# A new order of the same instructions in the five queues of a linear-attention and gMLP block

## The chip, the cores and the metric

The kernel runs on one core of one Trainium2 chip. The metric is the device time of one execution in microseconds (us), the median over runs. All times below are in us unless ns is written. The engines are PE (TensorE, matrix products), DVE (VectorE), ACT (ScalarE), POOL (GpSimd) and SP (SyncE, which here only issues DMAs).

## The reference

A residual block of linear attention is followed by a residual block of a spatial gMLP, in bf16. The sequence has 2048 rows of 512; 32 heads of 16; the gMLP is 1792 wide, in two halves of 896.

```
phi(t) = where(t > 0, t + 1, exp(t)) + 1e-6
q, k, v = heads(LN(x) @ wqkv);  pq, pk = phi(q), phi(k)
kv  = einsum('bhsd,bhse->bhde', pk, v);  z = sum over s of pk
o   = einsum('bhqd,bhde->bhqe', pq, kv) / (einsum('bhqd,bhd->bhq', pq, z) + 1e-6)
h   = x + o @ wo
u   = gelu(LN(h) @ w_in);  z1, z2 = u[:, :896], LN(u[:, 896:])
g   = w_sp @ z2 + b_sp            # 2048 x 2048 over the sequence
out = h + (z1 * g) @ w_out
```

## The kernel before, in words

**Program and order.** The kernel is written as a list of 1143 steps. A step is one instruction of DVE, ACT or POOL, one DMA issue, or a group of matmuls on PE. The helpers `matmuls`, `act`, `dve`, `pool`, `dma` and `dma_t` (a DMA that transposes) append steps; for each step the tiles that it reads and writes give the steps that must come before it. The order in which each engine runs its steps is not the order in which the code appends them. It stands in the constant `ORDER` (L16), a packed list of the 1143 step numbers written by an offline search. `schedule()` unpacks it and splits it by engine into five queues; each engine runs its queue strictly in order. `emit()` goes through the queues and writes, ahead of each step, the semaphore waits that its dependencies need and that no earlier step of the same engine has covered. So a step that waits holds up all that stand behind it on its engine. Because a helper records many steps, many rows of the profile have the helper's line: L413 is any group of matmuls, L432 any ACT instruction, L443 and L446 any load and any DMA transpose, L849 any sum of blocks (`comb`), L852 any `add_on`.

**SP's queue.** Of the 122 entries of SP's queue most are transposes (tiles of the normalized x into `xt6` to `xt15`, of the normalized h into `ht0` to `ht15`, of the spatial weights into `wt0` to `wt15` in two halves each, of the gated products into `zg0` to `zg15`). The others are loads (half of x, the wq, wv, wo, win2, win1 and wout weights), spreads of the reciprocals (`r`, in pieces) and stores (`o`). One `dma_t` occupies SP for some 1.2 to 1.3 us.

**Stages.** Times are those of the profiled execution.

- 0 to 8: loads of x, warm-up of PE.
- 8 to 50: attention. `k_unit` takes two tiles of 128 rows: statistics on DVE (`stats`), reciprocal root on POOL (`rstd`), `norm` on DVE or ACT (L566), transposes (on PE for tiles 0 to 5, on SP's queue for 6 to 15), the K projection and `phi` (an exp on ACT, then min and add, then max on DVE), and the accumulation of pk with xn (L670). `q_unit` does the same for 512 columns of Q (L413, then `phi`). Each of the two keeps its projections in pairs of PSUM banks.
- 43 to 61: the accumulated state `ct`, its product with wv (PE L753), the mask `kvm` (DVE L757) and the product with wo (`m`, L764). The denominators go through zc on PE, Ln and Exp on ACT, the spreads r on SP and the multiplication of pqT on DVE (L803). Four groups of 512 rows, tg = 0 to 3, follow each other.
- 57 to 72: h = x + pqT·m (DVE L815), squares on ACT, moments of a pair of tiles on POOL (`moments_pair`: L553 to L557), norm on DVE (L566), transposes ht on SP.
- 67 to 109: the first layer of the gMLP. `cell3` multiplies 2 x 2 blocks with seven products instead of eight: sums of weight blocks (`w_sums`: four for win2, four for win1), sums of blocks of hn (`hn_sums`), adds in PSUM by `add_on` (DVE L852) and gelu on ACT. z2 is normalized (moments on POOL at L545 to L548, the power at L561 or `rstd` at L529, norm at L566); `t1_sums` and `t_sums` make zt of it. `z1_tile` and `cell2` do the other half.
- 106 to 215: `mix`, eight times, is the spatial product with wt, again by seven products, with sums sa and wt (DVE L849), gate products (L984, L992) and the zg transposes. `cell2` lies between the first of them and `mo_pair`, the output product with wout (adds into h at DVE L1077), beside the later ones.
- 215 to 228.4: the last `mo_pair` and the stores.

Of the kernel before, what the change touches and what calls it, by code (L numbers as in the profile page):

```python
# [11 lines left out]
P = 128  # L12
GRAN = 16
EARLY = 0
SEM_NS = 45.0
ORDER = "c-jrpg8~@j0tV0z|7_c~ZQHhOw_44tc{SU%QA5qPS6j`h*4DPRd!ON)Scr|d0EqaAgXBmFBOQbkNRNObNQH<fh6pH%49JKyh=<}xi!4Zh)F^?HNQkT`g-j@ovdE0=sD*5(gSIG#D9C}j$c5UdhcZZnoG6d>$c+j}jQYrf{K$)TsE7{eh<s>(0;q&eXox~+jDo0)LFkM|Xo4h&jsX~mu4sxc&<s`41<g?fg)ta4&>ht<8A(wcU!ogoVj_B=1-`=9n1YsQg`PNqNf?4;n2KJQhC^71p@@nZ=#4)327NIdtuYL3FdWOV0wb^rt1%uwV<x`GNQ}Z^tid>}#X9uEFBpwkn1KG6gQNHX8!;Q3@GaJ31Lop5V&FT>!znDrd_=+`9K#qa!C0KYX)Hx#Y{nLx#2;9Ot$2uC*oNKMjy+g_g?NPhIDozQ5&Q5H&f*{*;|$JW2X^8-uHXVL;|4C`Dz4!YZXzb0;1;gqC7$9}+{P>1!9CnXWd4R|c!3RkjVSyR&#;DT`5YVh7veA~|3ggP$KQy{7<_<__y_A4oxdX<qwx(s{lCIHB;>zH%C~qAGZEu6Hk0u)K0u7c<Rk-=Fe0-v2MaI)3o-#CF(=EgBy%wp6SELgGdEK(9m}#5YcM5ivnJCs16MH(OS2A}GcEJ5F!M4qi?AH?u_(*46}xdIv#=O5F(d0TKP#{WTeBj2vO6oW7AvzQi?bf<vjlsv7ppNFzhoO`WdnZAZ}<;;^Dz5xJcsftwq;*7WOdGBI}YJ@Y|kp3z;F2@8?ghAa4vslKlbNrPUIX`<s>#`N6zCg4(BiYiEnv_T{xe&c#OAsh)3Cs$9b2(@*PKT0T=QFf8#+8;39TqW8ULQuIFOj=L25gQ@-a#PG%>b;w3)gM^53t9LdXU!p(fn!}`F^yuxI9LFfx!r9>syRQ|_N%%>z8%+VZ6>oX%LseWgEjbTbH;W$RrKt@tf3Kh^a{=rW?%~YDsmpsGNimX@~#2=VOv2~W26-C#$l-F5Ag%n3|^^gTsN`;k0Gx&;GHIvy?LQ%Dx#S~4=R8p_mTm#ia15{M;lwIf8RHap1W%WJNY8h9srM57>a;S_Rv4zU%F%zhjHnF^JFr5bJD^*u|B~%9GR0XwGbPds9-DDeeRz+=P4Sk_5%BAznsG9ndnY4|S^cUwVx4P<UeW_aNrbK$e;rd3qG*p#UTMM*P!!%cUG)i@}TYs~PMrwriXr9_CvEFdB_9}*AYC9LHyT)je7HS9Esje0)ua;<^R&%V{>zXEOsn)22Zm5T@>!zw|ijHWR#%ZeRsi$tKmu~Bw)@q&ZXuNi^nwIOJrs)^$VsG8mdfn3mb<}k2=C}G)^|e7W^qc<G3T@PPy01-Ypq2VwKj?S;p?|bloitNhG*Mf%hY$5YhxAx|v`UZkvsUYg`s$cY>ZqQopJu6{-U{BPy?m~He5MonsL$H27dox|Jgzf(ua}yw*E+xtqW7zjPN|6h(*>3AC!Ll2N`I=cF6x}@+Aiuj+M(dTRmcbQM*UUH#U06)bx9HYmm)isuPBCNI<^b@N1azmM|C{Maa>1n8ULjCPT)k2=!8z}22SGAj^?DU<4#WI<WA{wPT`uqs#N~P^<Bzoo!YgW#$|oPbsgR5T-hC*-WgrR8C>2KoXORk#T9+WSzXVKebAYm&4--bRbAaV+|ZqU!uNd49evVAeabm~#;4uLz1+mdoy&LK&0XBohyAm2`>b2JtGoN0&%1`d@d)?yNMG^=S8^Wbbu(XaK40`@_i<~t^)-L*fBe=xeAPpI)4%$<o4cJyxwqRmzkl<65A`iS@Ie3Juie7K{m66N*T4IrAA7X>`H7!-ko)_oUwD`c_y^DSbHDOS|LcN&=W%}R_a5vIUgy8v(qsIm2lz|3_eB5YkN#wY|NPkuF~e9-_ZObz%?=@Ah#daU6=r$7qlCC2LWmt^c&_7xSRqn~9-@T_jvqF8o)d?J;kIWwPFU{*AyG&YrZ{<+?1i4{ubeSt4oSl_rwrfvjW;-1ND~%0bx09Xg{)zXvxRgaeaIBPbIGvQ*+Y(yGc5KpZ*-Qh)wx5ikSEOd4lj59P%z{TMMB}Q(yN>=6bOaFHm`8;P&zDesj%G(yxLn_CKL;0L%Fcm4MX{`&pTZqR1OtGrBEdt@P6-djIi5P!wnY=)x%Qnam~;;Gz!(ikFF7#gxcXJ*9mn))KDv=4JAU;&@9vs^+JQtJoF4LLd(!Pv<iJfo6sw?4ShrV&@prgokP3OA!G=hLjTY`bPK)1fG{xh3tdBx@IT`6A!q"  # L16


class _Op:
# [13 lines left out]
class _Prog:  # L33
# [110 lines left out]
    def schedule(self):  # L144

        ids = np.frombuffer(zlib.decompress(base64.b85decode(ORDER)), np.uint16).tolist()
        assert len(ids) == len(self.ops)
# [981 lines left out]
```

## Time and profile before

| what | value |
|---|---|
| median of three runs | 230.19 us (229.83, 230.19, 230.55) |
| profiled execution | 230.16 us |
| its span in the trace | 228.4 us |
| outside the span | 1.76 us |
| granted PE clock | 1.00 throughout |
| transposes xnT<-xn, hnT<-hn, from issue to landing | 2.5 us, both (median) |
| load of win, 896 KB | 8.8 us (median of two) |
| spreads r<-rcp | 2.7 us |

The span is the time between the first and the last instruction of the program in the trace. A row of the timeline has the start in us, the length in us, the engine, the line, the operation, then the tile written and the tiles read with their sizes and, in brackets, how long the engine stood idle before it and what released it. The chain of waits is read back from the last instruction: at each step, what released it, or the instruction ahead of it on its engine. PE's idle time in it counts; that of an engine off the chain does not.

### The profile page before, as it was taken

The numbers are of one execution on the slowest core, as the hardware profiler recorded it, in microseconds if no ns is written. First come the engines' busy times: TensorE is split into PE (matmuls) and PEld (weight loads), VectorE is DVE, ScalarE is ACT, GpSimd is POOL, SyncE is SP. The second block draws the span as 40 slices with busy tenths as digits, with TensorE's granted clock in tenths as the row PEclk, the third lists the DMA queues.
The fourth block names the chain that finished last, engine by engine and source line by source line (L and its number), as shares of the span: only waits on it lengthen the run. The fifth ranks groups of instructions, "written<-read, shape, count | busy, mean of one in ns | idle before, by whom it ended". The sixth has DMA issues, their size and how long they took to land.

```text
span 228.4 us, 3524 instructions
## 1 busy us (share of the span) xinstructions
PE 221.4 (97%) x1253; PEld 115.3 (50%) x1253; DVE 177.8 (78%) x397; ACT 123.3 (54%) x232; POOL 49.7 (22%) x134
## 2 busy tenths in 40 slices
PE   7999999999999998999999999999999999999995
PEld 7444444453344443544545455555655556655553
DVE  3999656689999998999999955638877677553973
ACT  5794663489999998998654234425202213222111
POOL 2533600000567735595800000000000000000000
DMA  7725439957463337799980291249893150170664
GB/s 216 244 49 138 71 72 324 257 112 181 100 134 68 69 72 93 147 184 198 228 121 0 40 109 20 42 81 148 188 193 64 43 108 19 28 78 0 149 160 153
DMA packets 73905, 26.85 MB, mean 118 GB/s; under 512 B 63648, under 2 KB 73888, under 8 KB 73888
## 3 DMA queue, kind: packets, MB, share of 16 engines
q1 hardware_dynamic: 73184, 26.03, 56.0%
q10 hardware_dynamic: 704, 0.59, 0.8%
q8 instruction: 10, 0.16, 0.4%
q14 instruction: 7, 0.06, 0.1%
HBM read 6.95 MB, written 2.10 MB: 40 GB/s over the span
## 4 chain that ended last, share of the span: by engine, by line
PE 63%; DVE 12%; DMA 7%; ACT 7%; SPq 6%; POOL 3%; issue 2%; DVEq 0%
PE psum L413 57%; SPq L446 6%; PE psum L670 4%; DMA hnT<-hn 2%; DMA wt<-in_B_w_sp_dram 2%; DMA xnT<-xn 2%; ACT z L432 1%; DMA x<-in_A_x_dram 1%; DVE st L929 1%; DVE h L1077 1%; DVE pqT L803 1%; DVE h L815 1%; ACT xn L432 1%; ACT sq L432 1%; DVE psum L852 1%
## 5 line engine op out<-in xcount | busy, mean ns | idle before, releaser
L432 ACT ACTIVATE psum<-psum 128x448 f32<-128x448 f32 (+1 forms) x49 | 22.1, 464 | 57.7 <-PE psum L413 35.7
L413 PE MATMUL psum<-z,wt 128*128 128x448 bf16 x256 | 53.0, 353 | 0.0
L413 PEld LDWEIGHTS psum<-z,wt 128*128 128x128 bf16 x256 | 24.8, 98 | 22.1 <-DVE wt L849 0.6
L413 PE MATMUL psum<-win,hnT 128*128 128x448 bf16 x112 | 26.0, 352 | 1.0 <-DMA hnT<-hn 1.0
L413 PE MATMUL psum<-zt,sa 128*128 128x448 bf16 x128 | 26.7, 352 | 0.0
L432 ACT ACTIVATE z1t<-psum 128x448 bf16<-128x448 f32 (+1 forms) x24 | 16.1, 676 | 17.9 <-PE psum L413 17.2
L432 ACT ACTIVATE e<-psum 128x1024 bf16<-128x1024 f32 (+1 forms) x18 | 16.7, 927 | 13.1 <-PE psum L413 12.4
L852 DVE TENSOR_TENSOR psum<-psum,p5z 128x448 f32<-128x448 f32 x24 | 14.9, 624 | 5.8 <-ACT z1t L432 5.1
L413 PE MATMUL psum<-ws,hs 128*128 128x448 bf16 x72 | 18.9, 353 | 0.0
L413 PEld LDWEIGHTS psum<-zt,sa 128*128 128x128 bf16 x128 | 12.4, 98 | 11.0 <-DVE zt L849 0.4
L413 PEld LDWEIGHTS psum<-win,hnT 128*128 128x128 bf16 x112 | 10.8, 98 | 11.6 <-ACT z1t L432 1.7
L413 PE MATMUL psum<-wout,zgT 128*128 128x256 bf16 (+1 forms) x77 | 15.1, 302 | 0.8 <-DVE h L1077 0.7
L413 PE MATMUL psum<-xnT,wqkv 128*128 128x512 bf16 x64 | 15.5, 379 | 0.0
L984 DVE SCALAR_TENSOR_TENSOR z1t<-psum,b,z1t 128x448 bf16<-128x448 f32 x16 | 10.8, 682 | 5.8 <-PE psum L413 5.8
L413 PE MATMUL psum<-wqkv,xnT 128*128 128x512 bf16 x64 | 15.0, 379 | 0.2 <-DMA xnT<-xn 0.2
L432 ACT ACTIVATE z<-psum 128x896 bf16<-128x896 f32 x16 | 14.8, 944 | 0.6 <-PE psum L413 0.6
L670 PE MATMUL psum<-pk,xn 128*128 128x512 bf16 x64 | 15.1, 379 | 0.0
L413 PE MATMUL psum<-m,pqT 128*128 128x512 bf16 x64 | 14.6, 380 | 0.2 <-DVE h L815 0.2
L992 DVE TENSOR_TENSOR u<-psum,p 128x448 bf16<-128x448 f32 x16 | 9.9, 623 | 5.2 <-PE psum L413 5.1
L545 POOL TENSOR_SCALAR st<-st 128x1 f32<-128x1 f32 x10 | 4.2, 419 | 44.5 <-ACT sh L432 35.2
L592 DVE TENSOR_SCALAR e<-e 128x1024 bf16<-128x1024 bf16 (+1 forms) x18 | 7.2, 400 | 8.3 <-ACT e L432 8.1
L413 PE MATMUL psum<-zt,wt 128*128 128x448 bf16 x64 | 13.4, 352 | 0.0
(124 smaller groups left out, 384.4 us busy)
## 6 DMA issues: line engine op xcount, KB each, us to landing
r<-rcp SPq DMA_DIRECT2D x16, 128.0 KB, 2.7
out_dram<-h SPq DMA_DIRECT2D x15, 128.0 KB, 2.0
win<-in_B_w_in_dram SPq DMA_DIRECT2D x2, 896.0 KB, 8.8
x<-in_A_x_dram SPq DMA_DIRECT2D x6, 256.0 KB, 3.6
wqkv<-in_A_wqkv_dram SPq DMA_DIRECT2D x2, 512.0 KB, 4.4
wout<-in_B_w_out_dram SPq DMA_DIRECT2D x1, 896.0 KB, 6.5
wo<-in_A_wo_dram SPq DMA_DIRECT2D x1, 512.0 KB, 5.4
wt<-in_B_w_sp_dram SPq DMA_TRANSPOSE x32, 4.2
```

The lines of the kernel that those rows point to most:

```text
L413: inst = pe.matmul(out_ap, lhsT=a, rhs=b, start=start and i == 0, stop=stop and i == len(pairs) - 1, **kw)
L432: return g.add("ACT", lambda ac: ac.activation(out_ap, in_ap, func, **kw), [in_ap, *extra], [out_ap] + ([accum] if accum is not None else []),
L446: return g.add("SP", lambda q: q.dma_start_transpose(out_ap, in_ap), [in_ap], [out_ap], cost=issue, lat=lat, dma=name, **k)
L545: pool(lambda p: p.tensor_scalar(s[:, 2:3], s[:, 0:1], s[:, 0:1], -1.0 / (n * n), op0=ALU.mult, op1=ALU.mult), [s[:, 0:1]], [s[:, 2:3]], 240)
L592: dve(lambda v: v.tensor_scalar(e, e, 1.0, EPS_PHI, op0=ALU.min, op1=ALU.add), [e], [e], w * GW, acc=4)
L670: inst = pe.matmul(bank(CB[c]), lhsT=xn[:, i, c * P:(c + 1) * P], rhs=pk[:, i, :], start=i == 0, stop=i == NT - 1)
L803: dve(lambda v, q=q, r=r: v.tensor_tensor(q, q, r, ALU.mult), [q, r], [q], 2 * GW, acc=2)
L815: dve(lambda v, n=n, b=b, s=s: v.scalar_tensor_tensor(h[:, n, :], bank(b), 1.0, x[:, n, :], op0=ALU.mult, op1=ALU.add, accum_out=s[:, 0:1] ...
L852: dve(lambda v: v.tensor_tensor(half(b), half(src), p, ALU.add), [half(src), p], [half(b)], HW, ps=True)
L929: dve(lambda v, c=c, k=k: v.bn_stats(s[:, 6 * k:6 * k + 6], z2[:, n, c]), [z2[:, n, c]], [s[:, 6 * k:6 * k + 6]], HW)
L984: dve(lambda v: v.scalar_tensor_tensor(o, half(b), b32[:, n:n + 1], o, op0=ALU.add, op1=ALU.mult), [half(b), b32[:, n:n + 1], o], [o], HW, ...
L992: dve(lambda v: v.tensor_tensor(u, half(b), p, ALU.add), [half(b), p], [u], HW, ps=True)
```

## The change

Only the constant `ORDER` differs. The 1143 steps, their dependencies and their data are the same. The new list was found, by the words on the change, by a search on the mean of eight replays with random late transfers and longer vector work.

```diff
 SEM_NS = 45.0
-ORDER = "c-jrpg8~@j0tV0z|7_c~ZQHhOw_44tc{SU%
+ORDER = "c-jTQ0{|FQ00qE@Kijr#+qP}n4K>uv+G@6K
...
```

The two strings are shown by their first characters alone; what they unpack to is this. By engine, so many steps have another place in their queue: PE 163 of 306, DVE 313 of 381, ACT 99 of 204, POOL 111 of 130, SP 76 of 122. The first 17 and the last some 20 steps of PE's queue are the same. Most moves are by one to three places. The larger ones and those that touch a wait:

SP's queue, parts of it, from left to right (two halves of one transpose are written once, `a` and `b` where they are apart):

```
before: xt11 xt10 xt13 xt12 xt15 xt14 wv wo win2 win1 wt0 wt8
after:  xt10 xt11 xt12 xt13 xt15 wv wo win2 xt14 win1 wt0 wt8

before: ... r2 r2 r2 r2 bsp r31 r31 r30 r30 ht0 ht1 ht3
after:  ... r2 r2 r2 r2 r30 r30 r31 ht0 r31 ht1 ht3

before: ht4 ht6 ht9 ht10 ht11 ht8 ht13 ht12 ht14 ht15 wt1 wt9 wt2 wt10
after:  ht4 ht6 ht9 ht11 ht10 ht8 ht13 ht12 ht15 ht14 wt1 wt9 wt2a bsp wt2b wt10

before: wout wt7 wt15a zg0 wt15b zg1 zg8 zg9 wt4 wt12 wt5 zg10 zg2 wt13 wt6 wt14 zg3 o10 zg7 zg11 o80 zg15
after:  wout wt7a zg0 wt7b zg1 wt15 zg8 zg9 wt4 wt12 wt5 wt13 wt6a zg2 zg10 wt6b zg11 zg3 wt14 zg15 zg7 o20

before: zg14 o40 o20 o30 o150 o120 o110 o60 o140 o50 o130
after:  zg14 o30 o120 o40 o150 o10 o140 o60 o50 o130
```

DVE's queue (places in the queue, before and after):

```
step                               before  after
w_sums of win2, first two (426, 427) 71, 72   64, 65   now ahead of phi and zc
w_sums of win2, third (428)          76      67   now ahead of phi's max (217) and zc
w_sums of win2, fourth (429)        121      77   now ahead of L803, L815
w_sums of win1, third (432)         160      73   now ahead of kvm
kvm mask (243)                       74      75
statistics of tiles 12, 13     40/43/44/45   38 to 41
statistics of tile 14, 15            37/48   46/45
norm of tile 9 of hn (376)          129     129
norm of tile 8 of hn (374)          136     130   directly behind that of tile 9
norm of z2, step 500                175     158   now ahead of two add_on
hn_sums 509, 510, 511       131/137/134     134/135/136
```

ACT's queue: the norms of x for tiles 7, 9, 11, 13 and 15 and the copies ct each go one or two places ahead, past an exp of `phi`; the exp at step 260 goes one place ahead, past the reciprocals of tg = 2 (284); in the later stages the Identity steps p5 of `mix` and the copies change places by up to ten.

POOL's queue: the power for tiles 8 and 9 of hn (373) goes from place 73 to 70, the moments of z2 tiles (461, 487, 498, 499, 525) 3 to 16 places ahead, constants (ones32, sel) from places 36 and 38 to 9 and 12.

PE's queue: before the product of ct with wv (step 242, L753) there stands one step of `q_unit` less; between 74 and 130 steps of `z1_tile` and `cell3` change places by one to three; in `mix` the seven products of neighbouring calls are interleaved anew, by up to 18 places.

More of the change, by code (lines that the diff above doesn't have):

```diff
@@ L15 @@
 SEM_NS = 45.0
-ORDER = "c-jrpg8~@j0tV0z|7_c~ZQHhOw_44tc{SU%QA5qPS6j`h*4DPRd!ON)Scr|d0EqaAgXBmFBOQbkNRNObNQH<fh6pH%49JKyh=<}xi!4Zh)F^?HNQkT`g-j@ovdE0=sD*5(gSIG#D9C}j$c5UdhcZZnoG6d>$c+j}jQYrf{K$)TsE7{eh<s>(0;q&eXox~+jDo0)LFkM|Xo4h&jsX~mu4sxc&<s`41<g?fg)ta4&>ht<8A(wcU!ogoVj_B=1-`=9n1YsQg`PNqNf?4;n2KJQhC^71p@@nZ=#4)327NIdtuYL3FdWOV0wb^rt1%uwV<x`GNQ}Z^tid>}#X9uEFBpwkn1KG6gQNHX8!;Q3@GaJ31Lop5V&FT>!znDrd_=+`9K#qa!C0KYX)Hx#Y{nLx#2;9Ot$2uC*oNKMjy+g_g?NPhIDozQ5&Q5H&f*{*;|$JW2X^8-uHXVL;|4C`Dz4!YZXzb0;1;gqC7$9}+{P>1!9CnXWd4R|c!3RkjVSyR&#;DT`5YVh7veA~|3ggP$KQy{7<_<__y_A4oxdX<qwx(s{lCIHB;>zH%C~qAGZEu6Hk0u)K0u7c<Rk-=Fe0-v2MaI)3o-#CF(=EgBy%wp6SELgGdEK(9m}#5YcM5ivnJCs16MH(OS2A}GcEJ5F!M4qi?AH?u_(*46}xdIv#=O5F(d0TKP#{WTeBj2vO6oW7AvzQi?bf<vjlsv7ppNFzhoO`WdnZAZ}<;;^Dz5xJcsftwq;*7WOdGBI}YJ@Y|kp3z;F2@8?ghAa4vslKlbNrPUIX`<s>#`N6zCg4(BiYiEnv_T{xe&c#OAsh)3Cs$9b2(@*PKT0T=QFf8#+8;39TqW8ULQuIFOj=L25gQ@-a#PG%>b;w3)gM^53t9LdXU!p(fn!}`F^yuxI9LFfx!r9>syRQ|_N%%>z8%+VZ6>oX%LseWgEjbTbH;W$RrKt@tf3Kh^a{=rW?%~YDsmpsGNimX@~#2=VOv2~W26-C#$l-F5Ag%n3|^^gTsN`;k0Gx&;GHIvy?LQ%Dx#S~4=R8p_mTm#ia15{M;lwIf8RHap1W%WJNY8h9srM57>a;S_Rv4zU%F%zhjHnF^JFr5bJD^*u|B~%9GR0XwGbPds9-DDeeRz+=P4Sk_5%BAznsG9ndnY4|S^cUwVx4P<UeW_aNrbK$e;rd3qG*p#UTMM*P!!%cUG)i@}TYs~PMrwriXr9_CvEFdB_9}*AYC9LHyT)je7HS9Esje0)ua;<^R&%V{>zXEOsn)22Zm5T@>!zw|ijHWR#%ZeRsi$tKmu~Bw)@q&ZXuNi^nwIOJrs)^$VsG8mdfn3mb<}k2=C}G)^|e7W^qc<G3T@PPy01-Ypq2VwKj?S;p?|bloitNhG*Mf%hY$5YhxAx|v`UZkvsUYg`s$cY>ZqQopJu6{-U{BPy?m~He5MonsL$H27dox|Jgzf(ua}yw*E+xtqW7zjPN|6h(*>3AC!Ll2N`I=cF6x}@+Aiuj+M(dTRmcbQM*UUH#U06)bx9HYmm)isuPBCNI<^b@N1azmM|C{Maa>1n8ULjCPT)k2=!8z}22SGAj^?DU<4#WI<WA{wPT`uqs#N~P^<Bzoo!YgW#$|oPbsgR5T-hC*-WgrR8C>2KoXORk#T9+WSzXVKebAYm&4--bRbAaV+|ZqU!uNd49evVAeabm~#;4uLz1+mdoy&LK&0XBohyAm2`>b2JtGoN0&%1`d@d)?yNMG^=S8^Wbbu(XaK40`@_i<~t^)-L*fBe=xeAPpI)4%$<o4cJyxwqRmzkl<65A`iS@Ie3Juie7K{m66N*T4IrAA7X>`H7!-ko)_oUwD`c_y^DSbHDOS|LcN&=W%}R_a5vIUgy8v(qsIm2lz|3_eB5YkN#wY|NPkuF~e9-_ZObz%?=@Ah#daU6=r$7qlCC2LWmt^c&_7xSRqn~9-@T_jvqF8o)d?J;kIWwPFU{*AyG&YrZ{<+?1i4{ubeSt4oSl_rwrfvjW;-1ND~%0bx09Xg{)zXvxRgaeaIBPbIGvQ*+Y(yGc5KpZ*-Qh)wx5ikSEOd4lj59P%z{TMMB}Q(yN>=6bOaFHm`8;P&zDesj%G(yxLn_CKL;0L%Fcm4MX{`&pTZqR1OtGrBEdt@P6-djIi5P!wnY=)x%Qnam~;;Gz!(ikFF7#gxcXJ*9mn))KDv=4JAU;&@9vs^+JQtJoF4LLd(!Pv<iJfo6sw?4ShrV&@prgokP3OA!G=hLjTY`bPK)1fG{xh3tdBx@IT`6A!q"
@@ new lines @@
+ORDER = "c-jTQ0{|FQ00qE@Kijr#+qP}n4K>uv+G@6KqqeZsY@=px)x5UufY^u&A{OE!B_bj@j5tUKAs_;ZAQj>v1=6D!5+DsSAT^32BO)Oa(xNy@pd_-O6fz?#vY|8*qAaqb4r-wc%Aqb2AqQ%sEpnnfa-lu)ATjcy9de@sDj+iQAv*FS3F@IfDxv`jpdmV<6B?r+lA;m@p%4b3Gn$|>8et&5Ko?X&S2ROYG{;~J!DI|YcT`0+6h;e7MRl~qml%dAn1)vP7E#a*D={43p$2-QCYGZIR$)4NAu5t#2EIaXtUzn5#t0lj8?3?i7>Tv`0i)0dGtn30@HKwMER4r5_y+yZAHQNfe#2<Y!8#nq@0g7Vn21SOgvHp14LF7)n2SF!2AdEA$1xW7Fc0&w1xv6L%di={up3*k4STQv_pu#&u@KSl0Q+zN`*9Q}@gq*)6n5Yz9K>my!5Z$wd0fCnT)|bW<t3cOI-bL2TtiIU!b9A^BizKFc!B45iD!6>>xj%ve1g9bg&X)6qVgZyMjUSBQ>^D}{EN7JgFE;S@pu;>@e1$p0dEn5W=wv<XGCLcMrSN0CHM}Bn2=&J29gPwgz=f31(=*AnS&8nkP(@ag&2vsn42k?hh><UrI?DTnT|DBmU)?;wONz-SeQjvhs{}(8CaSrn1<!pise~>nV6AvnVD%>ku8{?-B^r0*_yRjoGaOeSvZ9C*pii4ncdloC0LF1nU!C%Eqn84R%bT;!YX{tuQ-(B*@Lq<i4!=S4LFQHvMMKXHrug1=durf<sA0qWX@whPT@~{!{69}*VvH#*@z=}g!9>y*Ey0m*pY|Wg@@UUzq2vB@+SY}TmHp^9Kb)=iKBRwQ~9%Q@oV1Z8Q$T0PUB;K!?Qfb%{<3<{FWanJ>gTH=NBBv4}8W8Y{F!M#_~8vvorr=ehntIfZs8R7BYf9(aNXfN~+IHsplNWh<d?Dy315r#OVw=!7;qZ0-C{>yu`)4$H+>d)Vj|fIEb+nTWOS8QB*`(^fwDBjtZ)%W-_amFs=$~IZNpzOQ@JmaVeuJo{B5JF0+{)aDcKYyGkmWnka!vtE~Rvzig_3YN-}#t{f_-D=ee$*-GVAT@RU7t+j%kHAv}{Qx%j@Z8TV4XsDv=D(7n%A2Ehb^Gnsx7N%EC4bw>FQU-NVB5h?%byY>>)(~yuE7npT)z&EO)Np;J?d+xz+NDaGs~!ACb+lXE^|eN8p4w`!dZ?}vYk@MVr&ckO7HN$3XrUHsipFY*@@lH;X`d=<jq2-?u4tNea;d7Qfp)Q%#;Lc~YBzsTJ6+azty6nV&@x@s9=_Fb_0cu$WmSEv75Yv$bY1J!K{s_!(=}1I^rtpxHUH8(%}_NR(rw+<Ms?IZ?c+*K(rZoD9euA=daq5ouOGBo5A{Y{^guJ!NvripTlGPQbyTy|SHG#DK5Cox^Rb?)pWy#=fWPXqo@l?0>4=_5Zlpi-NiX$Wb5z7H^tXOjA=^8&U9)vuCv;M$^si2<zalyKj2i17y;2O9@L8QxOvmy86?I9U7aiNhUE3E_%<&w@ab3#sUB`tT!KEG92^`Uh{G-Y^p%c5De^OFMbxmJXG?#TUC-HAi?)t9f6i(^NPUW;t?I`Z#G(PO|PUrN_=*G_A=+5Q_uIqZv<O<H>tj_Mt?(QRQ<b(d*P5p~=_>epJ4_EO~|Lo2_=5D^>CT``NKJF8)=!Wj<9zN+`eac_Cn!EV4tGc?IxubLWoO}9=n|ruhxV3Zprt|o$FF3C+`@GvYpDX#IuX&^|`A=VUTmR+TuHioJ<y*evVead@zUP5%=P&)*4?M{C{m|cgl*jlBKk;bi_ai^^2oLsSw|8%U?dg8%=Z+c1`K4cYj{Et&KX|hL@xSixAN<iR{nr1vfZzC&r+BtM8{r$z@(?o=^gG82Lp{^e9Ku+y@j4H1#Go+44w1un#|cqFgb*pj4c~gIGlytlg5!nxp684qdWatuI(A4L5`=^yQCROJAyY^imN|Kd8j^*z-r&tn5mJU!A$7R!@0=!V^F(j*a%T<MLi&&{Y;}yVz$?AcB}4YG!#P6kkTc{8bDbrua-OilTfE5mL&31!lbko~^=cOmi=8hN2t~p^UvZ&OHWUxV!V;GX<-$&v4;ey*P%#t@mBW5l3a`A&OTF8r!yZ=&4Z{JK2~|V&@S|&nYN1A`9qNQe;V0J$X+ynGKQs*uLfz0TG!HF8&(J!w3?)LV&?mGBjYE^rHna=v!{6>0dWF8BOXwUrgnpq@=pTBA?xAbw76ybKVPN<l`P(6A"
```

## The prediction

> **What bounds the kernel now.** First the page's share of each engine and its chain that ended last.
>
> ```profile
> PE 221.4 (97%) x1253; PEld 115.3 (50%) x1253; DVE 177.8 (78%) x397; ACT 123.3 (54%) x232; POOL 49.7 (22%) x134
> ...
> PE 63%; DVE 12%; DMA 7%; ACT 7%; SPq 6%; POOL 3%; issue 2%; DVEq 0%
> ```
>
> PE is busy for 221.4 of 228.4 us, and the change keeps every matmul. What an order can win is therefore only the time in which PE stands still. The shares of the other engines are means over stages, so the table of stages comes next: start and end, length, then PE, PEld, DVE, ACT and POOL, each with busy time and count, then clock, DMA share and GB/s.
>
> ```profile
> 50.00:61.00 11.00, 10.70 (x59) 3.97 (x55) 10.85 (x24) 10.38 (x17) 1.69 (x5) 1.00 0.62 146
> ...
> 74.00:90.00 16.00, 15.04 (x78) 6.83 (x77) 14.35 (x35) 15.76 (x29) 9.06 (x25) 1.00 0.47 76
> 90.00:104.50 14.50, 14.24 (x75) 6.82 (x72) 14.08 (x33) 13.96 (x27) 10.21 (x19) 1.00 0.85 163
> 104.50:120.00 15.50, 15.46 (x81) 7.62 (x82) 15.50 (x34) 9.99 (x19) 7.38 (x16) 1.00 0.95 179
> ```
>
> From 50 to 104.5 us DVE, ACT and PE are all above 90%; at 74 to 90 ACT is the fullest (15.76 of 16.00), at 104.5 to 120 DVE has no gap at all. A wait taken from PE there can come back as a wait for ACT or DVE. After 120 PE alone binds, and what it wins there stays won. The clock is 1.00 everywhere. Then PE's waits (us in total, times, longest):
>
> ```profile
> PE psum L413 <- DMA hnT<-hn: 1.0, 1, 1.0
> PE psum L413 <- DVE h L1077: 0.7, 2, 0.5
> ...
> PE psum L413 <- DVE psum L852: 0.3, 1, 0.3
> PE psum L413 <- DMA xnT<-xn: 0.2, 1, 0.2
> PE psum L413 <- DVE m L764: 0.2, 1, 0.2
> ```
>
> By the starts of PE's matmuls against their steady spacing (0.216 us for 512 columns, 0.189 for 448), the stalls after 21 us add up to 5.0 us: 0.37 at 21.04, 0.33 at 53.7, 0.67 in three between 55.8 and 61.1, 0.18 at 74.9 and 81.5, 1.12 at 89.10, 0.63 at 102.95 and 104.54, 0.27 in three between 115 and 127, 0.69 at 170.55, and 0.74 after 215, of which 0.54 lies in the last twenty PE steps, which keep their order. Everything this change can win is within about 4.4 us.
>
> The chain says what released the three largest (start, length, engine or transfer):
>
> ```profile
> 16.78 4.22 DMA xnT<-xn
> ...
> 84.45 4.52 DMA hnT<-hn
> ...
> 104.54 45.53 PE psum L413 x238
> ...
> 163.26 4.32 DMA wt<-in_B_w_sp_dram
> 170.55 45.35 PE psum L413 x277
> ```
>
> Two are transposes by DMA that took 4.2 and 4.5 us, where the page's median is 2.5 for both kinds. After 104.54 PE leads the chain for 45 us at a time.
>
> **The change, part by part.** Nothing is added or removed; all 1143 steps are placed anew within the five queues. I went along the new queues by hand with the durations of the old execution (230.16 us: 228.4 of span and 1.76 around it; the median is 230.19, so the sum stands for both).
>
> (a) 12 to 21 us. On ACT tile 7's norm goes ahead of a phi exp (1.0 us), so its transpose xt7, the load wq and the transpose xt8 issue 0.1 to 0.4 earlier. Before, wq issued at 16.15 and landed at 20.46, and xt8 issued at 16.78 and landed at 21.00, 0.54 behind it. PE's 0.37 ends with xt8. Ends: 0 and -0.37; I take -0.2, since xt8 hangs on wq, which moves 0.3.
>
> (b) xt14 goes behind the loads wv, wo and win2. Before it issued at 31.64, ahead of them; win2 issued at 34.05 and landed at 41.35. Now statistics and norms of tiles 12 to 15 come earlier on DVE and ACT, so xt15 can issue at 27.5, wv at 28.8 instead of 32.87, win2 near 30. By the same 7.3 us it lands near 37.3, and xt14 with it at 37.3 to 38.0. PE wants tile 14 at 39.0. Cost 0, cover 1 to 1.7 us; without the cover it is the slower rival below.
>
> (c) 43 to 67 us. Two more of the weight sums of `w_sums` (0.62 us each, rows of L849) come ahead of the multiplications by the reciprocals (L803) and the additions of x (L815), and ACT's exp at step 260 is placed ahead of the reciprocals of tg = 2, so the spreads r2 issue about 1.4 later (57.9 for 56.5). PE gets one step of kv·wo earlier (0.27 of new wait at 48.3), and the kvm mask 0.68 earlier, which takes the 0.33 at 53.7. Two sums fall into idle time of DVE (1.8 us at 43.0, 0.85 at 46.5), two (1.24) do not; against these stands the load bsp, 1.25 us of SP, which leaves the spreads. The ends: -0.1 (the old 0.33 goes and 0.27 comes) and +0.7 (half of the 1.24 lands on PE beside the 0.1 late r2). I take +0.3, the middle, since DVE's stage row (10.85 of 11.00) leaves no room.
>
> (d) 74 to 104.5 us, the largest. PE waits at 89.10 for the transpose ht8, issued fourth of its group (order ht9, ht10, ht11, ht8) at 84.45 because DVE's norm of tile 8 stands at 82.85. The new order takes POOL's power for tiles 8 and 9 about 1 us earlier, removes a weight sum from ahead of it on DVE, puts tile 8's norm just behind tile 9's (79.1) and sends ht9, ht11, ht10, ht8. So ht8 issues near 83.0 and by the usual 2.5 lands at 85.5 instead of 88.97: PE's 1.12 goes. What is late next is ACT:
>
> ```profile
> 89.68 0.53 ACT L432 ACTIVATE psum<-psum 128x448 f32<-128x448 f32 x1 [0.24 <-PE psum L413]
> ...
> 91.19 0.53 ACT L432 ACTIVATE psum<-psum 128x448 f32<-128x448 f32 x1 [0.54 <-PE psum L413]
> ```
>
> ACT's only idle time there, 0.24 and 0.54, is what can be closed up before ACT itself sets the pace: 0.78, not 1.12. Then the two waits for DVE's add (L852) at 102.95 and 104.54, 0.63 together: DVE is freed of two sums (1.24) and of its own idle 0.92 at 88.07, but stands at 14.08 of 14.50 and then without a gap, so I take half, 0.3. Together -1.1; ends -0.3 (ht8 stays late) and -1.75 (all of both).
>
> One rule speaks against this part. The row first: POOL's power L561 took 1.80 us at 100.97 against its usual 0.57, while DVE ran zt<-z2,z2, a sum of two tiles in SBUF, from 101.26 to 102.34.
>
> ```profile
> 100.97 1.80 POOL L561 TENSOR_TENSOR rs<-st,expo 128x1 f32<-128x1 f32 x1
> ```
>
> The Trainium skill, page "SBUF — State Buffer", section "Who interferes with whom", says that a DVE instruction with two SBUF inputs and a GpSimd instruction that reads SBUF share a port pair under an exclusive lock, so that one blocks the other for its whole length. The new order sets many powers elsewhere, between other DVE sums; by the rule any may take some 1.2 us more, by the usual row none. The power of that very row (525) moves nine places up, with 1.3 us before its norm, so that one such block is just hidden.
>
> (e) 104.5 to 150: stalls of 0.27 in three. DVE is without a gap until 132 and its new order serves the adds earlier by a step. Ends 0 and -0.27; I take -0.1. wt7 and wt15 stand behind zg0 and zg1 now (needed past 148, issued by 136): 0.
>
> (f) 150 to 200. At 170.55 PE waits 0.69 for L1077, held on DVE behind sums that waited for wt13, landed 167.58 (issue 163.26). The new queue of SP sends wt13 and the first half of wt6 before zg10 and zg2, so it lands near 164.9, and DVE does two L1077 first. wt14 goes behind zg11 and zg3, 4.2 later, wanted ten us after it lands. PE binds afterwards: -0.65, ends 0 and -0.69.
>
> (g) The end: the last twenty PE steps are the same. the step behind the 0.20 at 215.94 gets its inputs earlier, and SP has nine stores behind zg14, not ten, but o1 (stored at 180 before) is now among the last. 0, ends -0.2 and +0.2.
>
> Sum: -0.2 + 0 + 0.3 - 1.1 - 0.1 - 0.65 + 0 = -1.75, or 230.16 - 1.75 = 228.4. The best ends together (-0.37 - 0.1 - 1.75 - 0.27 - 0.69 - 0.2) are -3.4: 226.8. The worst without (b) are +0.6: 230.8.
>
> **Rivals.** *The late transpose stays late (229.2).* The 4.52 of ht8 ran beside 16 KB of instruction code in the DMA records at 85.39 and 87.24; other transposes beside such a fetch took 4.3 to 4.5 too (zg1 at 132.18). Issued at 83.0, ht8 lands before most of it, but ht13 or ht12 behind it may take its place. Part (d) then gives -0.3: -0.95 in all. Against it: the others of the group have several us of cover.
>
> *Nothing is gained (230.2).* The three measured runs differ by 0.3%, so lateness at random, which the new order is to bear, hardly occurs; and if in (c) and (d) every wait comes back from DVE or ACT (+0.7, -0.3) and (f) half, the sum is about 0.
>
> *Slower: xt14 waits behind the loads (231.3).* In the old order xt8, issued behind wq, landed 0.54 after it: the transpose waited for the load. If the loads are not earlier because norms of tiles 12 to 15 are held up, or because 1.9 MB drain no sooner, win2 lands at 41.35 as before and xt14 at 41.9. PE wants it at 39.0 and has nothing else to do: +2.9, and DVE and ACT (10.85 and 10.38 of 11.00 behind it) give nothing back: 228.4 + 2.9 = 231.3. It decides from a landing of 39.0 on; from 41.5 on the kernel is slower by over 0.3%.
>
> **How the numbers follow.** Chances: the forecast 0.40 (its own range 227.4 to 229.2), the late transpose 0.20, nothing gained 0.16, slower 0.24. A measurement of this kernel tells 0.3% (0.7 us) from no change: faster is under 229.5, slower over 230.9. Faster takes the forecast and nine tenths of the late transpose, 0.58; within 0.18; slower 0.24. The range goes from the best ends, 226.8, to the slower rival's 231.3.
>
> **What would show it.** Right: PE's wait for hnT at 89 gone, ht8 landed before 87, ACT without idle time at 89 to 92; no wait at 170 for L1077, wt13 landed by 166; xt14 landed before 39 and the chain's PE stretch from 21 unbroken past 44; stalls after 21 us near 3.3 instead of 5.0. Wrong: a PE wait for xnT at 39 to 42, a wait for the multiplications L803 or for L815 of more than 1 us at 57 to 64, or a new wait for ACT or POOL at 75 to 110 of the size of the old one.

## The result, and the profile after

The new order takes 228.83 us (median of six, 228.74 to 229.43), the old one 230.27 beside it (six, 229.83 to 230.75): a ratio of 0.994, 95% interval 0.9924 to 0.9957. That is 1.4 us faster; the forecast was 1.8 faster, 228.4. The profiled execution took 228.74, with a span of 227.0 and 1.74 around it. In some kernels below a single execution was disturbed and took 60 to 1100 us longer; such executions are left out, and two of these kernels (new_to_66 and xt14_first) have no usable trace for that reason.

The page of the new order, PE's and the other engines' shares and the chain that ended last:

```profile
PE 219.6 (97%) x1239; PEld 115.8 (51%) x1253; DVE 178.1 (78%) x397; ACT 123.3 (54%) x232; POOL 49.5 (22%) x134
...
PE 85%; DMA 4%; ACT 4%; DVE 3%; SPq 1%; issue 1%
```

PE's work is the same (14 matmul records are missing from this trace), but it now makes up 85% of the chain instead of 63%. The table of stages of the new order, columns as before:

```profile
50.00:61.00 11.00, 10.60 (x54) 3.99 (x54) 10.80 (x22) 10.25 (x17) 1.34 (x3) 1.00 0.56 129
61.00:74.00 13.00, 11.60 (x55) 5.21 (x54) 11.87 (x34) 10.93 (x30) 9.03 (x27) 1.00 0.43 95
74.00:90.00 16.00, 16.00 (x85) 7.78 (x83) 15.16 (x40) 15.80 (x32) 9.78 (x27) 1.00 0.41 83
90.00:104.50 14.50, 14.50 (x76) 6.71 (x74) 14.05 (x34) 14.50 (x28) 9.18 (x17) 1.00 0.71 142
```

From 74 to 104.5 PE no longer stands still: 16.00 of 16.00 and 14.50 of 14.50, where the old order had 15.04 and 14.24. But at 61 to 74 it has 11.60 of 13.00. The same stage of the old order had:

```profile
61.00:74.00 13.00, 12.90 (x62) 6.08 (x63) 12.74 (x39) 11.89 (x33) 9.01 (x27) 1.00 0.43 91
```

PE's waits in the new order name what came in:

```profile
PE psum L413 <- DVE pqT L803: 1.6, 2, 1.3
...
PE psum L580 <- DVE xn L566: 0.8, 3, 0.5
PE psum L413 <- DVE h L1077: 0.2, 1, 0.2
PE psum L413 <- issue: 0.2, 1, 0.2
PE psum L753 <- ACT ct L432: 0.2, 1, 0.2
```

The waits for hnT (1.0), for L852 (0.3) and for xnT (0.2) of the old order are gone, that for L1077 is down from 0.7 to 0.2, and a new one of 1.6 for the multiplications by the reciprocals has come. The chain of the new order around it:

```profile
56.20 1.05 ACT e L432
57.25 0.53 ACT rcp L432
...
57.79 0.54 SPq L778
58.38 0.60 SPq L778
59.03 0.60 SPq L778
59.67 4.15 DMA r<-rcp
63.85 1.30 DVE pqT L803 x2
65.20 2.33 PE psum L413 x10
```

ACT's exp (step 260) runs first, then the reciprocals of tg = 2 (step 284), then SP issues the four spreads r2 one after the other, and the last takes 4.15 us to land. A table shows where PE gained and lost. Both orders do the same matmuls, and at some points of the queue PE has done the same set in both; the start of the next one, against its start in the old trace, is how far PE is behind (+) or ahead (-) in us. The start in the old trace heads each column.

| kernel | 18.1 | 38.3 | 70.9 | 89.1 | 104.5 | 117.1 | 176.1 | 224.8 |
|---|---|---|---|---|---|---|---|---|
| the new order | +0.39 | +0.01 | +1.50 | +0.23 | -0.03 | -0.11 | -1.03 | -1.25 |
| r2_early | +0.77 | +0.39 | +1.04 | -0.22 | -0.42 | -0.50 | -1.43 | -1.64 |
| old_to_66 | +0.70 | +0.65 | +0.65 | -0.22 | -0.24 | -0.36 | -1.28 | -1.49 |
| new_from_117 | +0.01 | -0.06 | -0.06 | +0.10 | +0.11 | +0.11 | -0.65 | -0.86 |
| new_to_66_b | +0.76 | +0.48 | +1.87 | +1.87 | +1.24 | +1.23 | +0.89 | +0.89 |
| old_ht8 | +0.12 | +0.22 | +0.21 | +0.41 | +0.30 | +0.30 | -0.40 | -0.41 |
| old_wt13 | +0.36 | +0.51 | +0.50 | -0.11 | -0.12 | -0.12 | -0.83 | -0.83 |
| sums_old_place | +0.29 | -0.10 | +0.55 | -0.32 | -0.24 | -0.35 | -1.27 | -1.48 |
| sums_in_gap | -0.07 | -0.33 | +0.45 | -0.81 | -1.12 | -1.21 | -2.13 | -2.34 |
| r3_together | +0.05 | -0.31 | +0.10 | -1.17 | -1.36 | -1.45 | -2.37 | -2.58 |

The first column changes by up to 0.9 us between executions without regard to the order: outside the old trace itself (6.67) it rises with the landing of the load of x for tiles 4 and 5, issued at 2.18 in every trace and landed between 7.24 and 8.26. So rows are compared from 38.3 on. There the new order loses 1.49 up to 70.9, wins 1.53 up to 104.5 and another 1.22 to the end.

### The profile page after: what moved, and what is told of

Same layout as the page of the kernel before. It is cut to its first block, busy times and chain, and to the rows that moved or that the text cites. A ratio compares the mean times of both kernels' runs of the same rounds, so it can differ in the third digit from the quotient of the medians.

```text
span 227.0 us, 3520 instructions
## 1 busy us (share of the span) xinstructions
PE 219.6 (97%) x1239; PEld 115.8 (51%) x1253; DVE 178.1 (78%) x397; ACT 123.3 (54%) x232; POOL 49.5 (22%) x134
## 4 chain that ended last, share of the span: by engine, by line
PE 85%; DMA 4%; ACT 4%; DVE 3%; SPq 1%; issue 1%
PE psum L413 78%; PE psum L670 6%; DMA x<-in_A_x_dram 3%; DMA r<-rcp 2%; DVE st L521 1%; DVE h L1077 1%; ACT ct L432 1%; ACT e L432 1%; SPq L778 1%; DVE pqT L803 1%; SPq L443 1%; ACT rcp L432 1%; ACT r L432 0%; PE psum L753 0%; ACT pqT L432 0%
## 5 line engine op out<-in xcount | busy, mean ns | idle before, releaser
L432 ACT ACTIVATE psum<-psum 128x448 f32<-128x448 f32 (+1 forms) x49 | 22.9, 471 | 54.1 <-PE psum L413 37.1
L852 DVE TENSOR_TENSOR psum<-psum,p5z 128x448 f32<-128x448 f32 x24 | 15.0, 629 | 4.6 <-ACT z1t L432 4.0
L413 PE MATMUL psum<-xnT,wqkv 128*128 128x512 bf16 x61 | 15.0, 379 | 0.3 <-issue 0.2
L413 PE MATMUL psum<-wout,zgT 128*128 128x256 bf16 (+1 forms) x71 | 13.1, 295 | 0.4 <-DVE h L1077 0.2
L1077 DVE TENSOR_TENSOR h<-psum,h 128x256 bf16<-128x256 f32 x14 | 5.9, 420 | 9.1 <-remote 6.5
L521 DVE BATCH_NORM_STATS2 st<-x 128x6 f32<-128x512 bf16 x15 | 9.8, 681 | 3.8 <-DMA x<-in_A_x_dram 3.8
```

What stands on the lines that cost most here:

```text
L413: inst = pe.matmul(out_ap, lhsT=a, rhs=b, start=start and i == 0, stop=stop and i == len(pairs) - 1, **kw)
L432: return g.add("ACT", lambda ac: ac.activation(out_ap, in_ap, func, **kw), [in_ap, *extra], [out_ap] + ([accum] if accum is not None else []),
L521: dve(lambda v: v.bn_stats(s[:, 0:6], src[:, n, :]), [src[:, n, :]], [s[:, 0:6]], D)
L852: dve(lambda v: v.tensor_tensor(half(b), half(src), p, ALU.add), [half(src), p], [half(b)], HW, ps=True)
L1077: dve(lambda v, o=o, q=q, add=add: v.tensor_tensor(o, q, add, ALU.add), [q, add], [o], DH2, ps=True)
```

## The experiments

Two theories were set against each other. A: each stage counts for itself, so the late spreads cost 1.5 and the new order of 66 to 104.5 won 1.5. B: ACT and DVE set the pace from 50 to 104.5, and the new wait at 63.7 only stands in the place of the old ones at 89 and 104. In A a mended stage leaves the kernel 1.5 faster, in B it leaves it as it is. The ratios below are all against the old order, and each has its 95% interval behind it.

**r2_early.** The new order with one swap on ACT:

```diff
 283 Ln of the denominators, tg = 2
-260 exp of phi
 284 reciprocals, tg = 2
+260 exp of phi
```

> The new order with one swap on ACT: the reciprocals of tg = 2 (step 284) ahead of the exp of step 260, as in the old order, so that the four spreads r2 issue about 0.9 us earlier. Theory A (each stage counts for itself: the late r2 cost PE 1.5 us at 63.7, and the new order won 1.5 at 74 to 104.5 on its own account): PE's wait for L803 goes, 227.6 to 228.0, that is 0.9 to 1.2 below the new order's 228.8. Theory B (from 50 to 104.5 ACT and DVE set the pace, the wait at 63.7 only stands in the place of those at 89 and 104): PE's wait at 63.7 goes but waits of about 1 us come back between 75 and 105, 228.6 to 229.0.

228.17 us (six, 227.80 to 228.46), ratio to the old order 0.9911 (0.9891 to 0.9931), against 0.994 of the new order: 0.66 us less by the medians, between A and B (the two intervals overlap at their ends). PE's waits:

```profile
PE psum L413 <- DVE pqT L803: 0.6, 2, 0.3
```

The last r2 spread issued 0.37 earlier, at 59.30 (0.75 earlier against PE, which is 0.38 later at 38.3 here), landed at 61.91 after 2.61 us instead of 63.83 after 4.15. PE's loss from 38.3 to 70.9 falls from 1.49 to 0.65, and its gain from 70.9 to 104.5 stays (1.46): nothing is given back. On this point A holds. What remains of the loss, 0.65, is not the swap.

**old_to_66.** The old order of all queues up to 66 us, the new one behind it:

```diff
-five queues up to 66 us, new
+five queues up to 66 us, old (sums 429, 432 and load bsp in their old places too)
 five queues from 66 us, new
```

> The old order of all five queues up to 66 us (weight sums 429 and 432 and the load bsp in their old places too), the new order behind it. Theory A: the wait at 63.7 goes and the later gains stay, 227.2 to 227.6. Theory B: the gains at 89 to 104 do not come, since PE arrives 1.5 us earlier than ACT and DVE can serve it; 228.6 to 229.0.

228.48 (six, 228.09 to 228.62), ratio 0.9921 (0.9899 to 0.9943): 0.1 below what B gives and far from A. The table says why: nothing lost up to 70.9, but only 0.89 won up to 104.5, where the new order won 1.53. What came back is not a wait for ACT but, at 78.6, a stall of 0.43 for a weight sum in its old place (see sums_old_place below), so B has the time nearly right and the cause wrong. Its head gains nothing at xt8 either (see step (a) below).

**new_to_66**, and once more as **new_to_66_b** for a trace: the new order up to 66 us, the old one behind it.

```diff
-five queues up to 66 us, old
+five queues up to 66 us, new (sums 429, 432 and load bsp in their new places)
 five queues from 66 us, old
```

> The new order up to 66 us (with weight sums 429 and 432 and the load bsp in their new places), the old order behind it. Theory A: the late spreads cost their 1.5 us in full and nothing is won later, 231.5 to 231.9. Theory B: PE arrives later at the waits of 89 and 104, which shrink by as much, 230.1 to 230.5.

> The new order up to 66 us and the old one behind it once more, for the trace (the first one's profiled execution was disturbed). Its time was 231.05, 0.8 above the old order, between theory A (1.5) and B (0). Behind a wait of about 1.5 at 63.7, the waits at 89.1, 103 and 104.5 (1.76 in the old trace) should be smaller by 0.4 to 1.0.

231.05 (231.01 the second time), ratio 1.003 (1.0014 to 1.0046), 0.8 slower. The waits of PE in new_to_66_b:

```profile
PE psum L413 <- DVE pqT L803: 1.4, 2, 1.2
...
PE psum L413 <- DMA hnT<-hn: 1.0, 1, 1.0
```

The head loses 1.39 up to 70.9 and the wait for ht8 at 89 stays whole: SP issues the transposes ht later by as much as PE is late (ht9 at 82.37 for 80.58). Only the two waits for L852 near 103 and 104, 0.63 together, go: +1.87 at 89.1 becomes +1.24 at 104.5. So A holds for ht8 and B for the adds. It also shows that in the whole new order the wait for ht8 was won by the order behind 66, and not by PE's lateness. The size of that wait is not fixed, though: by the starts of PE's matmuls the old order behind 66 stalls there for 1.13 in the old trace, 1.18 here and 1.31 in new_from_117, but only 0.50 in old_wt13, whose queues up to that point are those of the old order; there ht8 landed after 3.91 instead of 4.52 to 4.70. So up to 0.6 of what the new order wins at 89 can be the luck of the one old trace.

**new_from_117.** The old order up to 117 us, the new one behind it.

```diff
 five queues up to 117 us, old
-five queues from 117 us, old
+five queues from 117 us, new
```

> The old order up to 117 us, the new one behind it: the parts from the spatial product on alone. By the trace of the new order PE stood level with the old one at 117 (0.1 ahead) and ended 1.25 ahead: both theories say 229.0 to 229.2, the wait for L1077 at 170.5 gone. If it is 229.6 or more, the gain behind 117 needs what comes before it.

228.96 (six, 228.58 to 229.17), ratio 0.9943 (0.9922 to 0.9963). The part behind 117 alone gives nearly all of what the whole change gives; everything ahead of it, taken together, comes out near nothing.

**old_wt13.** The old order with one move on SP.

```diff
 wt5
-zg10 zg2
 wt13
+zg10 zg2
 wt6
```

> The old order with one move on SP: the transposes wt13 ahead of zg10 and zg2, DVE's queue as it was. The forecast's step (f): wt13 lands near 164.9 and the sum that reads it no longer holds L1077 back, so the wait of 0.69 at 170.5 goes: 229.5 to 229.7. Rival: the order on DVE (two L1077 ahead of the sums) did it and SP's place alone does little: 229.9 to 230.4, with a wait at 170 of 0.3 or more.

229.60 (twelve, 228.60 to 230.11), ratio 0.9971 (0.9955 to 0.9986): 0.7 faster, as the forecast's step (f) says. wt13 landed at 164.16 and the sum that reads it, in its old place on DVE, waits for it no more:

```profile
166.37 0.42 DVE L1077 TENSOR_TENSOR h<-psum,h 128x256 bf16<-128x256 f32 x1 [1.88 <-remote]
166.71 0.68 DVE L849 TENSOR_TENSOR sa<-wt 128x1024 bf16<-128x1024 bf16 x1
```

The line of the sum has no bracket, where the old one had 0.68 of waiting for wt:

```profile
167.60 0.69 DVE L849 TENSOR_TENSOR sa<-wt 128x1024 bf16<-128x1024 bf16 x1 [0.68 <-DMA wt<-in_B_w_sp_dram]
```

PE's matmul of wout and zgT starts without a stall at 169.74. SP's place alone did it. With the old place the size of PE's stall varies: 0.69 in the old trace, 0.35 in new_to_66_b, and none in old_ht8, where wt13 landed at 167.58, 168.48 and 167.01. In the nine traces with the new place there is none.

**old_ht8.** The old order with tile 8 alone served earlier:

```diff
 DVE: 376 norm of tile 9
+     374 norm of tile 8
      ... six steps
-     374 norm of tile 8
 SP:  ht9
+     ht8
      ht10 ht11
-     ht8
```

> The old order with tile 8 alone served earlier: DVE's norm of tile 8 directly behind that of tile 9, and ht8 second of its group on SP (ht9, ht8, ht10, ht11). ht8 should land near 84.3 instead of 88.97. Theory A (ht8's lateness alone made the wait of 1.12 at 89): 229.1 to 229.4. Theory B (ACT and DVE set the pace there): the wait for hnT goes, but waits for ACT and DVE of about the same sum take its place before 105, 229.9 to 230.3. Between them, by the 0.78 of ACT's idle time: 229.5.

230.80 (twelve, 229.99 to 231.85), ratio 1.0027 (1.0007 to 1.0046): 0.3% slower, above both expectations. ht8 landed at 84.49, and the wait for hnT is gone, but:

```profile
PE psum L413 <- DVE hs L849: 1.0, 2, 0.7
```

```profile
88.58 0.55 PE L413 MATMUL psum<-ws,hs 128*128 128x448 bf16 x2 [0.73 <-DVE hs L849]
```

Now ht10 and ht11, third and fourth of the group, are the late ones: ht10 issued at 83.33 and landed at 87.65 after 4.33 us, ht11 issued at 84.64 and landed at 88.07 after 3.43. DVE stands idle for 1.46 us until ht11 is there, and its sum of hn blocks, which PE waits for, begins at 88.09. So one transpose of this group or two are late whatever their numbers, and moving the tile named by the wait moves the wait. Why the median is 0.46 above the old order's is not shown: the profiled execution, 230.32, is one of the faster ones, and in it PE gives back nothing but 0.09 from 70.9 to 104.5 and then wins the 0.70 at 170.5. The new order moves the steps around it as well.

**xt14_first.** The new order with xt14 back ahead of the loads.

```diff
 xt15
+xt14
 wv wo win2
-xt14
 win1
```

> The new order with one move on SP: the transpose xt14 back ahead of the loads wv, wo, win2. The forecast's step (b): xt14 behind the loads landed at 37.62 and PE took tile 14 at 39.2 without a wait, so the place costs nothing and the time stays 228.6 to 229.1, the same as the new order. Rival: the place was a gain (loads and with them the spatial weights come earlier); then it is slower, 229.3 or more.

229.10, with 228.83 and 228.95 beside it, ratio 0.9949 (0.993 to 0.9968): the same as the new order. The place costs nothing and wins nothing that shows.

**sums_old_place.** r2_early with two weight sums back:

```diff
 DVE, ahead of kvm and of m:
-432 and 429
 DVE, ahead of the add at 78, and near 93:
+429, and 432
```

> r2_early (the new order with the reciprocals of tg = 2 ahead of the exp) with the weight sums 429 and 432 back at their old places on DVE (before the add at 78, and near 93). In r2_early PE still lost 0.65 us between 50 and 66, and won 1.46 between 71 and 104.5; with the old order up to 66 it lost nothing there but won only 0.89 later. If the two sums (1.24 us of DVE) cause both, PE's loss at 50 to 66 falls below 0.3, a wait of about 0.4 appears at 78, and the time stays within 0.3 of r2_early's 228.2. If their early place is a gain by itself: 228.6 or more; if it is a loss: 227.8 or less.

228.68 (six, 228.22 to 228.99), ratio 0.9914 (0.9889 to 0.9939) against 0.9911 of r2_early; by the ratios they cannot be told apart. In the table PE loses the same 0.65 up to 70.9 (-0.10 to +0.55), so the two sums do not cause it, and a stall of 0.42 stands at 78.0, so that only 0.79 is won up to 104.5, where r2_early won 1.46. The early sums cost nothing ahead of 66 and are worth 0.67 behind it, by the traces.

**sums_in_gap and sums_in_gaps2.** r2_early with steps moved on DVE:

```diff
+431 weight sum
 243 kvm mask
-431 weight sum
 334 x added to h
+289 multiplication, tg = 2
-307 norm
 337 x added to h
-289 multiplication, tg = 2
 290 multiplication, tg = 2
+307 norm
```

and in sums_in_gaps2 also 432 from its place at 48 us to an idle stretch at 87.8.

> r2_early with the sum 431 moved on DVE ahead of the kvm mask, into an idle stretch of 0.71 us at 49.4, and the two multiplications L803 of tg = 2 one and two places ahead. If DVE's place in its queue is what holds L803 (63.4, when the reciprocals landed at 61.9), PE's wait of 0.51 at 64.0 and part of the 0.32 at 59.6 go: 227.6 to 227.9. If the time won comes back as waits for ACT between 74 and 105: 228.1 to 228.3.

> As sums_in_gap, and the sum 432 moved from 48 to DVE's idle stretch of 0.59 us at 87.8. If DVE's load ahead of L803 and L815 is what PE still pays for, 227.4 to 227.8; if ACT sets the pace at 74 to 105, 228.0 to 228.3, the same as r2_early.

228.29 (six, 227.68 to 228.52), ratio 0.9891 (0.9867 to 0.9915), and 228.22, ratio 0.9892 (0.9868 to 0.9916). Against r2_early's 0.9911 that decides nothing; both times lie where the second expectation put them (the time won comes back), and from 38.3 to the end PE gains 2.01 as against 2.03: no gain. The wait at 64 fell from 0.51 to 0.19, but one of 0.31 came at 68.2, as a row of DVE in sums_in_gap shows:

```profile
67.92 0.69 DVE L803 TENSOR_TENSOR pqT<-pqT,r 128x1024 bf16<-128x1024 bf16 x1 [0.27 <-DMA r<-rcp]
```

The last spread of r3 stands behind ht0 on SP, and ht0 waits for its norm. sums_in_gaps2 shows the same; 432's place makes no difference. So the gain came back, but from a spread on SP and not from ACT; neither theory had that wait in it.

**r3_together.** sums_in_gap with the old order of these two on SP:

```diff
 r31
-ht0
 r31
+ht0
 ht1
```

> sums_in_gap with the last spread of r3 on SP ahead of the transpose ht0, as in the old order. In sums_in_gap that spread stood behind ht0, which waited for its norm until 63.99; it issued at 65.24 and landed at 67.90, and PE waited 0.31 at 68.2. If PE alone pays for it the wait goes and PE ends 2.3 us ahead of the old order from 40 us on (sums_in_gap: 2.0): 227.7 to 228.1, ratio near 0.988. If ACT or DVE take the gain back before 105: the same time as sums_in_gap, 228.2 to 228.4, ratio 0.989 or more.

227.95 (five, 227.51 to 228.22), ratio 0.9902 (0.9876 to 0.9928). r31 landed at 66.09 instead of 67.90 and the wait is gone; from 38.3 to the end PE gains 2.27, where sums_in_gap gained 2.01 and the new order 1.26. The trace and the median are as expected of A; the ratio is not (0.988 was expected, and 0.989 or more if the gain is taken back), so that it beats sums_in_gap is shown by the trace alone. By the medians it is the fastest kernel, 0.9 below the new order, but the two intervals overlap at their ends (0.9876 to 0.9928 and 0.9924 to 0.9957). Clear of the new order's interval are sums_in_gap and sums_in_gaps2 alone.

## Why the forecast came out, step by step

| step | forecast | measured | by |
|---|---|---|---|
| (a) xt8 | -0.2 | -0.25 to -0.37 | PE from 18.1 to 21.0, seven traces |
| (b) xt14 | 0 | 0 | xt14_first |
| (c) 43 to 67 | +0.3, at most +0.7 | +1.49 | 38.3 to 70.9 |
| (d) 74 to 104.5 | -1.1, at most -1.75 | -1.53 | 70.9 to 104.5 |
| (e), (f) 104.5 to 200 | -0.75 | -1.00 | 104.5 to 176.1 |
| (g) the end | 0, at most -0.2 | -0.22 | 176.1 to 224.8 |
| sum | -1.75 | -1.44 | medians |

The direction was right, and the sum came close partly by luck: (c) cost 1.2 more than forecast, and (d) to (g) together won 0.9 more. The rows (c) to (g) add up to -1.26; what (a) won, the late load of x took in this trace. Of the signs that the forecast named, most came: no wait for hnT at 89, none for L1077 at 170, wt13 landed by 166 and xt14 before 39, ACT without idle time from 89 to 92. ht8 before 87 did not (88.67), and one that it had named as a sign of being wrong did: PE waited for the multiplications L803 by more than 1 us (1.51 up to 65.20).

**(a)** Right in what it won. In seven traces that have the new head PE makes up 0.25 to 0.37 between 18.1 and 21.0; in four besides the old one that have the old head it makes up at most 0.07 or loses up to 0.15. In the trace of the new order the late load of x ate the gain (+0.39 to +0.02), and wq and xt8 issued no earlier than before, at 16.27 and 17.03.

**(b)** Right, with its numbers: wv issued at 29.15, win2 at 30.32, landed at 37.20, and xt14 landed at 37.62, within the 37.3 to 38.0 of the forecast. PE took tile 14 at 39.19 without a wait. The slower rival, that xt14 waits behind 1.9 MB and lands at 41.9, did not come, and the cover of 1 to 1.7 us was 1.57.

```profile
30.32 0.51 SPq L443 DMA_DIRECT2D win<-in_B_w_in_dram  x1
30.87 1.20 SPq L446 DMA_TRANSPOSE xnT<-xn  x1
32.12 0.58 SPq L443 DMA_DIRECT2D win<-in_B_w_in_dram  x1
```

**(c)** This step failed. It put "the 0.1 late r2" beside "half of the 1.24" of the weight sums. The two sums cost nothing here (sums_old_place), and the late spreads cost 0.84. The issue was forecast nearly rightly, r2 at 57.79 (57.9 in the forecast) and the last at 59.67 where the old order had 58.42; but a price of 0.1 leaves room only for the usual 2.7 us from issue to landing. What was missed is that the spread now ran beside a fetch of instruction code, 16 KB in the DMA records at 61.55, and landed after 4.15 us; of its 16 parts the last came 1.5 later than the last but one (63.83 and 62.30). In the old order the fetch fell at 60.80 on the load bsp, which stood behind r2 and which nobody wanted (3.79 us to landing, where the same load takes 2.3 in its new place). The forecast had seen such a lateness in its rival for ht8 (where the second record, at 87.24, is one of 8 KB and not 16) and did not ask it of r2. Of the 1.49 the swap on ACT explains 0.84. The other 0.65 are waits of 0.1 to 0.5 between 53 and 64, seen in every kernel with the new order there, of which r3_together still has 0.41; what makes those was not separated.

**(d)** Right in sign and in size within its ends, partly for another reason. The wait for ht8 went, but ht8 did not come early: issued at 84.49, landed at 88.67, 4.18 us after, against 85.5 in the forecast. The rival "late transpose" was right on the lateness and wrong on the price: PE, late from 63.7, arrived at 89.33. That lateness is not what saved it, since in r3_together, where PE is level at 86.5 (0.04 ahead), ht8 lands at 87.34 and PE takes it at 87.93:

```profile
87.93 0.35 PE L413 MATMUL psum<-win,hnT 128*128 128x448 bf16 x1
```

No bracket: no wait. There the order serves ht8 1.6 earlier than the old one (87.34 for 88.97), which leaves 0.59 to spare. The cap of 0.78 from ACT's idle time was too low: PE got 1.13 back at 89.1 at once, and ACT then ran full (14.50 of 14.50) without PE waiting for it. The two waits for L852 go where PE comes 1.9 late to them (new_to_66_b) and stay where it comes 0.1 early (old_wt13, 0.62 together); of the 1.53, 0.89 came without the early weight sums (old_to_66), the rest with them (0.67 in r2_early against sums_old_place).

The lengthening that spoke against this part came again, but not everywhere. In the new order DVE's sum zt<-z runs while POOL's power of step 560 runs (97.62 to 99.40, 1.78 us); the power ends 0.41 after the sum, and DVE's next norm waits for it:

```profile
97.90 1.09 DVE L849 TENSOR_TENSOR zt<-z 128x1792 bf16<-128x1792 bf16 x1
99.44 0.51 DVE L566 TENSOR_SCALAR z<-z,st,rs 128x896 bf16<-128x896 bf16 x1 [0.45 <-POOL rs L529]
```

So the victim was another power than the forecast named (525), at the same price, 1.8 for 0.6 to 0.7, and DVE waited 0.45 for it while PE did not. But in the same trace the next power that meets such a sum, from 104.05 with the sum from 104.36, took its usual 0.55, and the old trace has the like (0.57 from 104.03); the POOL instruction behind it then took 0.84 and ended 0.08 after the sum. So two instructions that overlap are not enough for the price of 1.2 that the forecast put on any power. That they interfere agrees with the Trainium skill, page "SBUF — State Buffer", section "Who interferes with whom", which gives the two a shared port pair with an exclusive lock; by the trace's starts it was the POOL power, begun 0.28 ahead of the sum, that was held up. No run here takes the lock apart.

**(e), (f), (g)** Right, and a little past their best ends (-1.00 for -0.96, -0.22 for -0.2). The small waits between 115 and 127 are gone with the 0.69 at 170.5 and the 0.20 at 215.94; wt13 landed at 164.50, forecast 164.9. (f) was priced from one trace and one edit (old_wt13) confirms it, though the old wait was anything from 0 to 0.69; that the trace it was priced from had the largest of them is luck.

## What to carry to other kernels

When a transfer is moved, ask of its new time what every late row of the old trace was late beside, and not only of the transfer that the wait names: beside a fetch like the one that ht8 was late beside, r2 came late. In a stage where three engines are full, price the steps of the queue that releases PE and leave the idle share of the others out; a wait moved away from one tile came back at its neighbour (old_ht8) and a wait at another spread (sums_in_gap) until the order of the whole group was changed. And where a stage behind is bound by one engine alone, its gain can be taken as whole: the part behind 117 gave what it promised, alone (new_from_117) and with the rest.

## What the runs showed of the hardware

Two things were not expected. A fetch of 16 KB of instruction code came up at nearly the same place of PE's work in every trace (60.7 to 61.9 and 85.0 to 87.2 us) and took 0.9 to 1.5 us. Taken over all twelve traces, every spread r, transpose ht and load bsp that SP had issued 0.70 to 2.05 us ahead of such a fetch was late, landing after 3.4 to 4.7 us instead of 2.4 to 3.1, and none that was issued 2.13 us ahead or more. From 1.5 us ahead nearly always only the last part was late (ht8 in the new order: last but one 86.98, last 88.67), nearer to the fetch all of them (ht8 in the old order, 0.95 ahead: from 88.39 to 88.97, after 4.52). The last r2 of the new order was 1.88 ahead and late, that of r2_early 2.17 ahead and not. So less than 0.1 us (2.05 against 2.13) can decide whether a transfer is hit, and in all twelve traces ht8 or, in old_ht8, ht10 and ht11 were. That the fetch and the transfers share the engines of the DMA is argued from this pattern; no run took the fetch away. And the load of x for tiles 4 and 5 landed up to 1.6 us apart (6.67 to 8.26) in executions of kernels that issue it alike, and PE stood up to 0.9 us apart at 18 us; that is more than the order changed in most stages.
